# One double-width GpSimd multiply per split unit, in-place even part, bf16 broadcast row

## The chip, the cores and the metric

The kernel runs on one core of a Trainium2 chip. The metric is the device time of one execution in microseconds (us). The core's engines are TensorE (PE in the profile; PEld is its weight load), VectorE (DVE), ScalarE (ACT), GpSimd (POOL) and SyncE (SP, which issues DMAs here). GpSimd works only between SBUF tiles; matmul results lie in PSUM, which VectorE and ScalarE read.

## The reference, cut to what matters

```python
# x: 8 x 3008 x 256; w_gate, w_val: 256 x 1536; w_out: 1536 x 256; all float32
X = np.fft.fft(x, axis=1)
X = np.fft.fft(X, axis=2)
h = X.real.astype(np.float32).reshape(8 * 3008, 256)
g = h @ w_gate
silu = g * (1.0 / (1.0 + np.exp(-g)))
out = (silu * (h @ w_val)) @ w_out
```

The real part of a 2D Fourier transform of real data has a symmetry: row k and row 3008 - k of a batch are the sum and the difference of an even part and an odd part. The kernel computes the two parts once and forms both rows ("plus" and "minus") from them.

## The kernel before, in words

The transform along the sequence is done with matmuls against cosine and sine tables. Its input is first folded to a quarter of its length on GpSimd (`fold_steps`, lines 153 to 172), and the transform's results are put by VectorE (line 580, `put`) into bf16 tiles `Pt` (even part) and `Qt` (odd part). The transform along the 256 columns is multiplied into the weights beforehand (`Wp`, `Wq`, `Wm`).

The columns (sequence positions of all batches) are cut into 24 tiles `t`, of 480, 512 and at the end 320 columns; the hidden width 1536 is cut into 12 slices `f` of 128. A unit is a pair (t, f). All units run in order, and the order on every engine is the order in which the program is written (`manual_schedule`). A turn of the main loop writes `part_a` of a unit, four matmuls of the output stage, `part_b` of the unit before, four more of the output stage, and then what is due there of the folds on GpSimd and of the transforms (`whole_part`).

There are two kinds of unit. In a plain unit, TensorE builds gate `g` and value `v` of the plus rows in PSUM, ScalarE takes the SiLU (line 743), VectorE multiplies (line 744); in `part_b` a further matmul into the same banks turns both into the minus rows, and ScalarE and VectorE repeat the step (lines 761 and 762). In a split unit the value is left as even part `e` and odd part `o`, in two PSUM banks, and VectorE makes both signs from them in three steps: `es` = e plus the broadcast row `bc` times a column of `w0` (line 731), `vp` = es - o/2 (line 733), `vm` = es + o/2, written backwards (line 735). The multiply of SiLU and value is then GpSimd's: the plus rows in `part_a` (line 736), the minus rows in `part_b` (line 758), each behind ScalarE's SiLU of that sign (lines 728 and 757). `bc` is row d=0 of `Qt` spread over all partitions by a matmul, once for each tile (lines 855 to 859).

Tiles 3 to 22 have split units: f = 0, 2, 3, 5, 7, 9 in tiles 3 to 20, and f = 0, 1, 2, 4, 5, 7, 8, 10, 11 in tiles 21 and 22. That makes 126.

The products go to the bf16 tiles `hp` (plus) and `hm` (minus). The output stage (`OWork`, line 676) of a tile starts when its last unit is done and is spread over the next tile's units, eight matmuls to a unit: first the blocks of plus rows, each over f = 0 to 11, then those of minus rows. ScalarE copies the result to `ev`, SyncE writes it out.

PSUM has three banks for `g` (`psG`), three for `v`, `e` and `o` (`psV`), and two for the output stage (`psO`). A bank is free for the next matmul when its last reader is done: for `e` that is line 731, for `o` line 735. In SBUF, the pools `sgv` (SiLU) and `vv` (`vp` and `vm`) have four single buffers each, and `es` two.

Of the kernel before, what the change touches and what calls it, by code (L numbers as in the profile page):

```python
# [12 lines left out]
F32 = mybir.dt.float32  # L13
I32 = mybir.dt.int32
BF16 = mybir.dt.bfloat16
AF = mybir.ActivationFunctionType
Alu = mybir.AluOpType
# [14 lines left out]
def kernel(  # L32
# [8 lines left out]
    nc = tc.nc  # L41
    B, M, D = x.shape
    Dff = moe_w_gate.shape[1]
    P = 128
# [4 lines left out]
    nF = Dff // P  # L49
    T = 512  # L50
# [16 lines left out]
    def width(t):  # L67
        return wide[t]
# [17 lines left out]
    Wo = const.tile([P, nF, D], BF16, name="Wo")  # L86
# [3 lines left out]
    w0 = const.tile([P, nF], F32, name="w0")  # L90
# [169 lines left out]
    for i in range(6):  # L260
        ps = psO.tile([P, T], F32, name="o")
# [252 lines left out]
    def pq_tiles(t):  # L514
        if t not in ptile:
            w = width(t) + B if t == nT - 1 else T
            ptile[t] = (pqp if t < nT - 1 else const).tile([P, w], BF16, name="Pt")
            qtile[t] = (pqp if t < nT - 1 else const).tile([P, w], BF16, name="Qt")
        return ptile[t], qtile[t]
# [94 lines left out]

    hp = ctx.enter_context(tc.tile_pool(name="ht", bufs=2))
    sgp = ctx.enter_context(tc.tile_pool(name="sg", bufs=3))
    sgv = ctx.enter_context(tc.tile_pool(name="sgv", bufs=4))
    esp = ctx.enter_context(tc.tile_pool(name="es", bufs=2))
    bcp = ctx.enter_context(tc.tile_pool(name="bc", bufs=2))
    vvp = ctx.enter_context(tc.tile_pool(name="vv", bufs=4))  # L620
    evp = ctx.enter_context(tc.tile_pool(name="evO", bufs=4))

    def row_pieces(c0, n, minus):


        res = []
        c = c0
        while c < c0 + n:
            if c >= NC:
                res.append((c - c0, c0 + n - c, (c - NC) * M, M))  # L630
                break
            b, r = divmod(c, H)
            for lo, hi, k0 in ((0, GH, 4), (GH, G, H), (G, G + GH, 2), (G + GH, 2 * G, H + 2),
                               (2 * G, 3 * G, 1), (3 * G, 4 * G, H + 1)):
                if lo <= r < hi:
                    break
            e = min(c0 + n, b * H + hi)
            k = k0 + 4 * (r - lo)
            if minus:
                res.append((c0 + n - e, e - c, b * M + M - k - 4 * (e - c - 1), 4))  # L640
            else:
                res.append((c - c0, e - c, b * M + k, 4))
            c = e
        return res

    def rows(r0, n, step):
        return out[r0:r0 + step * (n - 1) + 1:step, :]

    class OWork:
# [21 lines left out]
        def run(self, k):  # L671
            for st, pair, j, minus, c, n, f, hts, t in self.steps[:k]:
                if "ps" not in st:
                    st["ps"] = psO.tile([P, 2, D], F32, name="o")
                ps = st["ps"]
                nc.tensor.matmul(ps[:n, j, :], hts[minus][:, f, c:c + n], Wo[:, f, :],  # L676
                                 start=(f == 0), stop=(f == nF - 1))
                if j == len(pair) - 1 and f == nF - 1:
                    ev = evp.tile([P, 2, D], F32, name="ev")
                    np_ = max(q[2] for q in pair)  # L680
                    if all(q[2] == P for q in pair):
                        nc.scalar.copy(ev[:, 0:len(pair), :], ps[:, 0:len(pair), :])  # L682
                    else:
                        for jj, q in enumerate(pair):
                            nc.scalar.copy(ev[:q[2], jj, :], ps[:q[2], jj, :])
                    for jj, (mi, cc, nn) in enumerate(pair):
                        for p0, cnt, r0, step in row_pieces(t0[t] + (width(t) - cc - nn if mi else cc), nn, mi):
                            nc.sync.dma_start(out=rows(r0, cnt, step),
                                              in_=ev[p0:p0 + cnt, jj, :])
            self.steps = self.steps[k:]  # L690

    units = [(t, f) for t in range(nT) for f in range(nF)]
    hts = {}
    state = {}
# [6 lines left out]
    bc = {}  # L701
# [5 lines left out]
    def part_a(u):  # L707
        t, f = u
        w = width(t) + (B if t == nT - 1 else 0)
        fs = slice(f * P, (f + 1) * P)  # L710
        if f == 0:
            hts[t] = (hp.tile([P, nF, T + B], BF16, name="hp"), hp.tile([P, nF, T], BF16, name="hm"))
        Pt, Qt = pq_tiles(t)

        def mm(ps, Wt, gv, src, start, stop):
            nc.tensor.matmul(ps[:, :w], Wt[:, gv, fs], src[:, :w], start=start, stop=stop,  # L716
                             skip_group_check=True)

        g = psG.tile([P, T], F32, name="g")
        mm(g, Wp, 0, Pt, True, False)  # L720
        mm(g, Wq, 0, Qt, False, True)
        if split(u):
            e = psV.tile([P, T], F32, name="v")
            mm(e, Wp, 1, Pt, True, True)
            o = psV.tile([P, T], F32, name="v")
            mm(o, Wm, 1, Qt, True, True)
            sg = sgv.tile([P, T], F32, name="sgv")
            nc.scalar.activation(sg[:, :w], g[:, :w], AF.Silu)  # L728
            stt = nc.vector.scalar_tensor_tensor
            es = esp.tile([P, T], F32, name="es")  # L730
            stt(es[:, :w], bc[t][:, :w], w0[:, f:f + 1], e[:, :w], op0=Alu.mult, op1=Alu.add)  # L731
            vp = vvp.tile([P, T], F32, name="vv")
            stt(vp[:, :w], o[:, :w], -0.5, es[:, :w], op0=Alu.mult, op1=Alu.add)  # L733
            vm = vvp.tile([P, T], F32, name="vv")
            stt(vm[:, w - 1::-1], o[:, :w], 0.5, es[:, :w], op0=Alu.mult, op1=Alu.add)  # L735
            nc.gpsimd.tensor_tensor(hts[t][0][:, f, :w], sg[:, :w], vp[:, :w], op=Alu.mult)  # L736
            state[u] = (g, vm)
            return
        v = psV.tile([P, T], F32, name="v")
        mm(v, Wp, 1, Pt, True, False)  # L740
        mm(v, Wq, 1, Qt, False, True)
        sg = sgp.tile([P, T], F32, name="sg")
        nc.scalar.activation(sg[:, :w], g[:, :w], AF.Silu)  # L743
        nc.vector.tensor_tensor(hts[t][0][:, f, :w], sg[:, :w], v[:, :w], op=Alu.mult)  # L744
        state[u] = (g, v)

    def part_b(u):
        t, f = u
        w = width(t)
        Pt, Qt = pq_tiles(t)  # L750
        g, v = state.pop(u)
        for gv, ps in ((0, g), (1, v))[:1 if split(u) else 2]:
            nc.tensor.matmul(ps[:, :w], Wm[:, gv, f * P:(f + 1) * P], Qt[:, :w], start=False, stop=True,  # L753
                             skip_group_check=True)
        if split(u):
            sg = sgv.tile([P, T], F32, name="sgv")
            nc.scalar.activation(sg[:, w - 1::-1], g[:, :w], AF.Silu)  # L757
            nc.gpsimd.tensor_tensor(hts[t][1][:, f, :w], sg[:, :w], v[:, :w], op=Alu.mult)  # L758
            return
        sg = sgp.tile([P, T], F32, name="sg")  # L760
        nc.scalar.activation(sg[:, :w], g[:, :w], AF.Silu)  # L761
        nc.vector.tensor_tensor(hts[t][1][:, f, w - 1::-1], sg[:, :w], v[:, :w], op=Alu.mult)  # L762


    slot = {(b, part): max(first_tile[(b, part)] - 1, 0) * nF + 4 for b, part in jobs}
# [10 lines left out]
    for b in range(2, B, 2):  # L776
        u = slot[(b, 0)] - 1
# [41 lines left out]
    for jb in jobs[1:]:  # L819
        u = slot[jb]  # L820
# [30 lines left out]
    for i, u in enumerate(units):  # L851
        t, f = u
        if f == 0 and split((t, SPLIT[0])):
            ps = psG.tile([P, T], F32, name="g")
            w = width(t)
            nc.tensor.matmul(ps[:, :w], sel, pq_tiles(t)[1][:, :w], start=True, stop=True)  # L856
            bc.pop(t - 2, None)
            bc[t] = bcp.tile([P, T], F32, name="bc")
            nc.scalar.copy(bc[t][:, :w], ps[:, :w])
        for fn in before.pop(i, ()):  # L860
            fn()
        if i == 10:
            loads[0:0] = ((("A", 1), fn) for fn in load_a(1, nc.sync))
        run_loads(3)
        part_a(u)
        if owork:
            owork.run(4)
        if prev is not None:
            part_b(prev)
            if prev[1] == nF - 1:  # L870
                owork = OWork(prev[0], hts[prev[0]])
                owork.run(4)
        if owork and not (prev is not None and prev[1] == nF - 1):
            owork.run(4)
        for what, j in fold_at.get(i, ()):
            fold_step(what, j, i)
        for what in act_at.pop(i, ()):
            load_next(what)
        if i in job_at:
            whole_part(*job_at[i])  # L880
        prev = u
# [35 lines left out]
```

## Time and profile before

| what | value |
|---|---|
| time, median of 3 runs | 688.46 us (687.03, 688.46, 688.67) |
| span of the profiled execution | 685.5 us |
| PE busy | 672.8 us, 98% of the span |
| POOL busy | 579.1 us, 84% |
| DVE busy | 514.6 us, 75% |
| ACT busy | 432.9 us, 63% |
| DMA | 52.55 MB, 77 GB/s on average |

The span runs from the first to the last instruction of one profiled execution. The profiled execution's own time is not listed apart from the three runs; their median lies 3.0 us above the span. A row of the timeline gives the start in us, the duration in us, the engine, the line of the kernel, the operation, output<-input with shapes, and how many equal instructions in a row; in brackets, how long the engine had stood idle before it and what released it. A row of the groups gives the number of instructions, their busy time in us and the mean of one in ns, then the idle time before them. In the rows of the stages stand the stretch, its length, and the busy time of PE, PEld, DVE, ACT and POOL with the number of instructions, the granted clock, the DMA share and GB/s.

### The profile page before, as it was taken

What the parts mean: (1) busy time and instruction counts of PE and PEld (TensorE: products, weight loads), DVE (VectorE), ACT (ScalarE), POOL (GpSimd) and SP (SyncE); (2) the same over time, 40 slices, a digit from 0 to 9 for tenths busy, and PEclk for the clock granted to TensorE, in tenths of its full rate; (3) what the DMA queues carried; (4) which work ended last, traced back from release to release, by engine and by line L of the source; (5) the groups of instructions that cost most, each with busy time, mean ns of one, the idle gap of its engine ahead of it and who ended that gap; (6) DMA issues with size and microseconds to landing.
All of it is one profiled execution on the core that took longest, in us unless ns stands there. A gap on an engine that the chain in (4) does not pass through costs nothing.

```text
span 685.5 us, 13259 instructions
## 1 busy us (share of the span) xinstructions
PE 672.8 (98%) x4374; PEld 414.2 (60%) x4374; DVE 514.6 (75%) x919; ACT 432.9 (63%) x764; POOL 579.1 (84%) x565
## 2 busy tenths in 40 slices
PE   8999999999999999999999999999999999999997
PEld 5446655666656566565665566655665656656676
DVE  8896667777777777777777777777786777788862
ACT  7676655666656666565666666655665656656663
POOL 8897987899998999999998989997999555658920
PEclk9999999999999999999999999999999999999999
DMA  9657353324315213335134111125111111101112
GB/s 220 115 77 133 102 138 113 96 76 101 99 32 134 67 51 105 86 71 131 41 76 116 48 32 47 47 58 128 46 48 32 38 40 33 47 31 47 47 48 70
DMA packets 45567, 52.55 MB, mean 77 GB/s; under 512 B 6290, under 2 KB 33466, under 8 KB 45498
## 3 DMA queue, kind: packets, MB, share of 16 engines
q1 hardware_dynamic: 42314, 49.35, 27.4%
q0 software_dynamic: 3184, 2.36, 2.7%
q8 instruction: 34, 0.56, 0.4%
q14 instruction: 35, 0.29, 0.2%
HBM read 29.39 MB, written 24.65 MB: 79 GB/s over the span
## 4 chain that ended last, share of the span: by engine, by line
PE 89%; DVE 5%; issue 2%; POOL 2%; ACT 0%; DVEq 0%; ACTq 0%; POOLq 0%
PE o L676 34%; PE v L716 17%; PE g L716 16%; PE g L753 9%; PE v L753 4%; PE g L567 3%; PE v L567 3%; DVE vv L735 3%; DVE vv L733 1%; PE v L543 1%; PE g L543 1%; PE g L856 1%; PE g L421 1%; PE v L421 1%; PE o L430 0%
## 5 line engine op out<-in xcount | busy, mean ns | idle before, releaser
L736 POOL TENSOR_TENSOR hp<-sgv,vv 128x512 bf16<-128x512 f32 (+1 forms) x126 | 160.1, 1272 | 54.3 <-DVE vv L733 42.4
L676 PE MATMUL o<-Wo,hp 128*128 128x256 bf16 (+2 forms) x1140 | 169.7, 273 | 0.0
L676 PE MATMUL o<-Wo,hm 128*128 128x256 bf16 (+2 forms) x1140 | 169.7, 273 | 0.0
L758 POOL TENSOR_TENSOR hm<-sgv,vv 128x512 bf16<-128x512 f32 (+1 forms) x126 | 159.6, 1272 | 8.5 <-ACT sgv L757 8.1
L676 PEld LDWEIGHTS <-hp 128*128 128x128 bf16 (+2 forms) x1140 | 111.9, 98 | 68.3 <-issue 7.8
L676 PEld LDWEIGHTS <-hm 128*128 128x128 bf16 (+2 forms) x1140 | 111.8, 98 | 64.8 <-issue 4.9
L744 DVE TENSOR_TENSOR hp<-sg,v 128x512 bf16<-128x512 f32 (+2 forms) x162 | 107.9, 666 | 33.2 <-ACT sg L743 32.4
L731 DVE SCALAR_TENSOR_TENSOR es<-bc,w,v 128x512 f32<-128x512 f32 (+1 forms) x126 | 93.7, 744 | 50.5 <-PE v L716 50.3
L762 DVE TENSOR_TENSOR hm<-sg,v 128x512 bf16<-128x512 f32 (+2 forms) x162 | 107.4, 663 | 24.1 <-ACT sg L761 14.4
L761 ACT ACTIVATE sg<-g 128x512 f32<-128x512 f32 (+2 forms) x162 | 94.7, 585 | 45.6 <-PE g L753 45.4
L743 ACT ACTIVATE sg<-g 128x512 f32<-128x512 f32 (+2 forms) x162 | 94.4, 583 | 45.0 <-PE g L716 43.5
L716 PE MATMUL g<-Qt,Wq 128*128 128x512 bf16 (+2 forms) x288 | 108.0, 375 | 0.5 <-DVE Qt L580 0.5
L716 PE MATMUL g<-Pt,Wp 128*128 128x512 bf16 (+2 forms) x288 | 108.1, 376 | 0.1
L716 PE MATMUL v<-Pt,Wp 128*128 128x512 bf16 (+2 forms) x288 | 108.0, 375 | 0.0
L753 PE MATMUL g<-Qt,Wm 128*128 128x512 bf16 (+2 forms) x288 | 108.0, 375 | 0.0
L757 ACT ACTIVATE sgv<-g 128x512 f32<-128x512 f32 (+1 forms) x126 | 75.3, 598 | 47.4 <-PE g L753 41.1
L728 ACT ACTIVATE sgv<-g 128x512 f32<-128x512 f32 (+1 forms) x126 | 75.1, 596 | 40.3 <-PE g L716 35.5
L733 DVE SCALAR_TENSOR_TENSOR vv<-v,es 128x512 f32<-128x512 f32 (+1 forms) x126 | 87.0, 690 | 17.6 <-PE v L753 1.0
L735 DVE SCALAR_TENSOR_TENSOR vv<-v,es 128x512 f32<-128x512 f32 (+1 forms) x126 | 85.7, 680 | 2.7 <-POOL hm L758 2.7
L716 PEld LDWEIGHTS <-Wp 128*128 128x128 bf16 x576 | 56.2, 98 | 41.0 <-issue 4.2
L682 ACT COPY ev<-o 128x512 f32<-128x512 f32 x90 | 52.7, 586 | 30.8 <-PE o L676 28.2
L153 POOL TENSOR_TENSOR SDf<-XA 128x1024 f32<-128x1024 f32 x28 | 66.0, 2364 | 5.2 <-DMA XC<-in_x_dram 3.3
(165 smaller groups left out, 738.0 us busy)
## 6 DMA issues: line engine op xcount, KB each, us to landing
out_dram<-ev SPq DMA_DIRECT2D x96, 128.0 KB
XA<-in_x_dram SPq DMA_DIRECT2D x32, 256.0 KB
XA<-in_x_dram SPq DMA_DIRECT2D x112, 64.0 KB
XC<-in_x_dram SPq DMA_DIRECT2D x32, 120.0 KB
XC<-in_x_dram SPq DMA_DIRECT2D x105, 32.0 KB
out_dram<-ev SPq DMA_DIRECT2D x12, 120.0 KB
out_dram<-ev SPq DMA_DIRECT2D x10, 112.0 KB
XA<-in_x_dram SPq DMA_DIRECT2D x1, 1024.0 KB
```

The lines of the kernel that those rows point to most:

```text
L676: nc.tensor.matmul(ps[:n, j, :], hts[minus][:, f, c:c + n], Wo[:, f, :], start=(f == 0), stop=(f == nF - 1))
L716: nc.tensor.matmul(ps[:, :w], Wt[:, gv, fs], src[:, :w], start=start, stop=stop, skip_group_check=True)
L731: stt(es[:, :w], bc[t][:, :w], w0[:, f:f + 1], e[:, :w], op0=Alu.mult, op1=Alu.add)
L733: stt(vp[:, :w], o[:, :w], -0.5, es[:, :w], op0=Alu.mult, op1=Alu.add)
L735: stt(vm[:, w - 1::-1], o[:, :w], 0.5, es[:, :w], op0=Alu.mult, op1=Alu.add)
L736: nc.gpsimd.tensor_tensor(hts[t][0][:, f, :w], sg[:, :w], vp[:, :w], op=Alu.mult)
L743: nc.scalar.activation(sg[:, :w], g[:, :w], AF.Silu)
L744: nc.vector.tensor_tensor(hts[t][0][:, f, :w], sg[:, :w], v[:, :w], op=Alu.mult)
L753: nc.tensor.matmul(ps[:, :w], Wm[:, gv, f * P:(f + 1) * P], Qt[:, :w], start=False, stop=True, skip_group_check=True)
L758: nc.gpsimd.tensor_tensor(hts[t][1][:, f, :w], sg[:, :w], v[:, :w], op=Alu.mult)
L761: nc.scalar.activation(sg[:, :w], g[:, :w], AF.Silu)
L762: nc.vector.tensor_tensor(hts[t][1][:, f, w - 1::-1], sg[:, :w], v[:, :w], op=Alu.mult)
```

## The change

- `hp` and `hm` become one tile `hpm` with an axis for the sign.
- `sg` and `vv` of a split unit hold both signs in one tile, with three such buffers each (before: four single ones).
- GpSimd multiplies both signs in one instruction of 2 x 512 columns, in `part_b`. Only for f = 10 and 11 (split in tiles 21 and 22 alone) the plus rows keep an instruction of their own in `part_a`.
- The pool `es` is gone: the even part is written to the plus half of `vv`; then the minus half is made from it, and then the plus half in place. The minus step thus comes second and the plus step third.
- `bc` is bf16 instead of float32.
- Output buffers `ev`: three instead of four.

Line numbers behind the edits fall by one or two: 731 becomes 730, 733 and 735 become 732 and 731 (plus and minus change places), 758 becomes 757, 676 becomes 675.

```diff
-    sgv = ctx.enter_context(tc.tile_pool(name="sgv", bufs=4))
-    esp = ctx.enter_context(tc.tile_pool(name="es", bufs=2))
+    sgv = ctx.enter_context(tc.tile_pool(name="sgv", bufs=3))
...
-    vvp = ctx.enter_context(tc.tile_pool(name="vv", bufs=4))
-    evp = ctx.enter_context(tc.tile_pool(name="evO", bufs=4))
+    vvp = ctx.enter_context(tc.tile_pool(name="vv", bufs=3))
+    evp = ctx.enter_context(tc.tile_pool(name="evO", bufs=3))
...
-                nc.tensor.matmul(ps[:n, j, :], hts[minus][:, f, c:c + n], Wo[:, f, :],
+                nc.tensor.matmul(ps[:n, j, :], hts[:, minus, f, c:c + n], Wo[:, f, :],
...
-            hts[t] = (hp.tile([P, nF, T + B], BF16, name="hp"), hp.tile([P, nF, T], BF16, name="hm"))
+            hts[t] = hp.tile([P, 2, nF, T], BF16, name="hpm")
...
-            sg = sgv.tile([P, T], F32, name="sgv")
-            nc.scalar.activation(sg[:, :w], g[:, :w], AF.Silu)
+            sg = sgv.tile([P, 2, T], F32, name="sgv")
+            nc.scalar.activation(sg[:, 0, :w], g[:, :w], AF.Silu)
             stt = nc.vector.scalar_tensor_tensor
-            es = esp.tile([P, T], F32, name="es")
-            stt(es[:, :w], bc[t][:, :w], w0[:, f:f + 1], e[:, :w], op0=Alu.mult, op1=Alu.add)
-            vp = vvp.tile([P, T], F32, name="vv")
-            stt(vp[:, :w], o[:, :w], -0.5, es[:, :w], op0=Alu.mult, op1=Alu.add)
-            vm = vvp.tile([P, T], F32, name="vv")
-            stt(vm[:, w - 1::-1], o[:, :w], 0.5, es[:, :w], op0=Alu.mult, op1=Alu.add)
-            nc.gpsimd.tensor_tensor(hts[t][0][:, f, :w], sg[:, :w], vp[:, :w], op=Alu.mult)
-            state[u] = (g, vm)
+            vv = vvp.tile([P, 2, T], F32, name="vv")
+            stt(vv[:, 0, :w], bc[t][:, :w], w0[:, f:f + 1], e[:, :w], op0=Alu.mult, op1=Alu.add)
+            stt(vv[:, 1, w - 1::-1], o[:, :w], 0.5, vv[:, 0, :w], op0=Alu.mult, op1=Alu.add)
+            stt(vv[:, 0, :w], o[:, :w], -0.5, vv[:, 0, :w], op0=Alu.mult, op1=Alu.add)
+            if f >= nF - 2:
+                nc.gpsimd.tensor_tensor(hts[t][:, 0, f, :w], sg[:, 0, :w], vv[:, 0, :w], op=Alu.mult)
+            state[u] = (g, (sg, vv))
             return
...
-            sg = sgv.tile([P, T], F32, name="sgv")
-            nc.scalar.activation(sg[:, w - 1::-1], g[:, :w], AF.Silu)
-            nc.gpsimd.tensor_tensor(hts[t][1][:, f, :w], sg[:, :w], v[:, :w], op=Alu.mult)
+            sg, vv = v
+            nc.scalar.activation(sg[:, 1, w - 1::-1], g[:, :w], AF.Silu)
+            m = slice(1 if f >= nF - 2 else 0, 2)
+            nc.gpsimd.tensor_tensor(hts[t][:, m, f, :w], sg[:, m, :w], vv[:, m, :w], op=Alu.mult)
             return
...
-            bc[t] = bcp.tile([P, T], F32, name="bc")
+            bc[t] = bcp.tile([P, T], BF16, name="bc")
```

More of the change, by code (lines that the diff above doesn't have):

```diff
@@ L743, in part_a @@
         nc.scalar.activation(sg[:, :w], g[:, :w], AF.Silu)
-        nc.vector.tensor_tensor(hts[t][0][:, f, :w], sg[:, :w], v[:, :w], op=Alu.mult)
+        nc.vector.tensor_tensor(hts[t][:, 0, f, :w], sg[:, :w], v[:, :w], op=Alu.mult)
         state[u] = (g, v)
@@ L761, in part_b @@
         nc.scalar.activation(sg[:, :w], g[:, :w], AF.Silu)
-        nc.vector.tensor_tensor(hts[t][1][:, f, w - 1::-1], sg[:, :w], v[:, :w], op=Alu.mult)
+        nc.vector.tensor_tensor(hts[t][:, 1, f, w - 1::-1], sg[:, :w], v[:, :w], op=Alu.mult)
     slot = {(b, part): max(first_tile[(b, part)] - 1, 0) * nF + 4 for b, part in jobs}
```

## The prediction

> **What bounds the kernel now.** I read the page first: busy shares, granted clock, the chain that ended last.
>
> ```profile
> span 685.5 us, 13259 instructions
> PE 672.8 (98%) x4374; PEld 414.2 (60%) x4374; DVE 514.6 (75%) x919; ACT 432.9 (63%) x764; POOL 579.1 (84%) x565
> PEclk9999999999999999999999999999999999999999
> PE 89%; DVE 5%; issue 2%; POOL 2%; ACT 0%; DVEq 0%; ACTq 0%; POOLq 0%
> PE o L676 34%; PE v L716 17%; PE g L716 16%; PE g L753 9%; PE v L753 4%; PE g L567 3%; PE v L567 3%; DVE vv L735 3%; DVE vv L733 1%; PE v L543 1%; PE g L543 1%; PE g L856 1%; PE g L421 1%; PE v L421 1%; PE o L430 0%
> ```
>
> TensorE at full clock sets the time. The change leaves every matmul and its order alone, so it can only move the moments at which TensorE waits. One other line stands out in the chain: `vv L735`, the third VectorE step of a split unit. I then asked the stages, since the change is on GpSimd.
>
> ```profile
> 120.00:420.00 300.00, 298.62 (x1937) 182.87 (x1935) 230.43 (x403) 190.33 (x335) 288.84 (x266) 1.00 0.30 79
> 540.00:600.00 60.00, 59.81 (x393) 37.03 (x391) 45.92 (x82) 38.98 (x68) 33.21 (x27) 1.00 0.14 41
> ```
>
> The last busy column before the clock is POOL: 96% while folds run (tiles 3 to 13), 55% behind them. POOL is close to the bound in the middle, and PE (the first column) is as full there as later. Last I looked in the timelines for the place where L735 meets TensorE, in tile 9, units f=2 and f=3.
>
> ```profile
> 274.02 0.38 PE L716 MATMUL v<-Pt,Wp 128*128 128x512 bf16 x1
> 274.24 0.38 PE L716 MATMUL v<-Qt,Wm 128*128 128x512 bf16 x1
> ...
> 276.19 0.38 PE L716 MATMUL v<-Pt,Wp 128*128 128x512 bf16 x1
> 276.67 0.38 PE L716 MATMUL v<-Qt,Wm 128*128 128x512 bf16 x1
> ```
>
> ```profile
> 274.44 0.75 DVE L731 SCALAR_TENSOR_TENSOR es<-bc,w,v 128x512 f32<-128x512 f32 x1 [0.73 <-PE v L716]
> 275.32 0.69 DVE L733 SCALAR_TENSOR_TENSOR vv<-v,es 128x512 f32<-128x512 f32 x1
> 275.93 0.68 DVE L735 SCALAR_TENSOR_TENSOR vv<-v,es 128x512 f32<-128x512 f32 x1
> 276.53 0.68 DVE L762 TENSOR_TENSOR hm<-sg,v 128x512 bf16<-128x512 f32 x1
> 277.12 0.74 DVE L731 SCALAR_TENSOR_TENSOR es<-bc,w,v 128x512 f32<-128x512 f32 x1
> ```
>
> Two split units stand side by side. Matmuls start 0.22 us apart (274.02, 274.24), but f=3's odd matmul comes 0.48 behind its even one: it needs the bank of f=2's odd part, free when L735 ends (275.93 + 0.68 = 276.61). So 0.26 us is lost, and the chain behind it starts with the even matmul at 274.02 and runs through all three VectorE steps without slack. The same gap is in each of tiles 3 to 20 once (f=2, 3) and six times in tiles 21 and 22: 24 in all, of which these are the first and the last.
>
> ```profile
> 111.98 0.36 PE L716 MATMUL v<-Pt,Wp 128*128 128x480 bf16 x1
> 112.39 0.36 PE L716 MATMUL v<-Qt,Wm 128*128 128x480 bf16 x1
> ...
> 650.77 0.38 PE L716 MATMUL v<-Pt,Wp 128*128 128x512 bf16 x1
> 651.25 0.38 PE L716 MATMUL v<-Qt,Wm 128*128 128x512 bf16 x1
> ```
>
> These 24 stalls, about 6 us, are nearly all that TensorE loses behind the start, and most that any change here could win.
>
> **The change, part by part.** First VectorE. The three steps stay three and the odd bank is still freed by the third; but that step now writes the even row in place, after the second has read it. In the built program it waits for the second's semaphore, where before both only read `es`. I need the price of such a wait.
>
> ```profile
> 5.90 1.37 DVE L306 SCALAR_TENSOR_TENSOR rr<-kf,mM,t 128x377 f32<-128x377 f32 x2
> 7.31 0.82 DVE L310 TENSOR_SCALAR ra<-rr 128x754 int32<-128x754 int32 x1
> ```
>
> L310 waits directly for the L306 in front of it and starts 0.04 us after its end (5.90 + 1.37 = 7.27). L735, with no such wait, starts 0.08 before the end of L733 (275.32 + 0.69 = 276.01, against 275.93). So the wait costs 0.12 us. The upper bound is the existing es-to-vv step, 275.32 against 274.44 + 0.75 = 275.19: 0.13 behind the end, so 0.21. I take 0.12, since L310's is the same single wait; es-to-vv waits for several things.
>
> On this, the Trainium skill's page "VectorE: DVE Perf Modes", section "The DRAIN you can't avoid", says that a semaphore between VectorE instructions costs nothing extra, as the pipeline drains anyway. The rows above disagree; by it this term would be nothing.
>
> Second, the first step. It writes `vv` directly, so it waits for GpSimd (the product three split units back) as well as for the matmul: a separate wait instruction comes in front. A VectorE step with such a pair, L580, against PE:
>
> ```profile
> 282.87 0.49 PE L567 MATMUL g<-Tab,BBc 64*128 64x376 bf16 x2
> ...
> 283.47 0.61 DVE L580 TENSOR_TENSOR Qt<-g,od 128x304 bf16<-128x304 f32 x2 [0.62 <-PE g L567]
> ```
>
> It starts 0.11 us after the matmuls' end; the es row above started 0.04 after its own (274.02 + 0.38 = 274.40). So I take 0.06 more, bounds 0 and 0.09 (the 0.13 of es-to-vv, less 0.04). Behind the waiting step stand the rest of VectorE's queue and, through the banks, TensorE; with three double buffers the product it needs is three split units old, so GpSimd itself rarely holds it.
>
> Both lie on the chain of the 24 pairs: 24 x (0.12 + 0.06) = 4.3 us, bounds 24 x 0.12 = 2.9 and 24 x (0.21 + 0.09) = 7.2. In the other 102 split units the 0.18 is hidden: VectorE idles before a later step (0.73 us in the 274.44 row). Were that cover gone they would cost as much each, 18 us.
>
> Third, the bf16 row.
>
> ```profile
> L744 DVE TENSOR_TENSOR hp<-sg,v 128x512 bf16<-128x512 f32 (+2 forms) x162 | 107.9, 666 | 33.2 <-ACT sg L743 32.4
> L731 DVE SCALAR_TENSOR_TENSOR es<-bc,w,v 128x512 f32<-128x512 f32 (+1 forms) x126 | 93.7, 744 | 50.5 <-PE v L716 50.3
> L733 DVE SCALAR_TENSOR_TENSOR vv<-v,es 128x512 f32<-128x512 f32 (+1 forms) x126 | 87.0, 690 | 17.6 <-PE v L753 1.0 <-POOL hp L736 0.3
> L735 DVE SCALAR_TENSOR_TENSOR vv<-v,es 128x512 f32<-128x512 f32 (+1 forms) x126 | 85.7, 680 | 2.7 <-POOL hm L758 2.7
> ```
>
> One bf16 side beside f32 ones brings nothing (L744, 666 ns, against 680 and 690): 0 for L731, and 0 for the copy that writes `bc`.
>
> Fourth, GpSimd: 126 + 126 products become 122 double ones and four pairs.
>
> ```profile
> L736 POOL TENSOR_TENSOR hp<-sgv,vv 128x512 bf16<-128x512 f32 (+1 forms) x126 | 160.1, 1272 | 54.3 <-DVE vv L733 42.4
> L758 POOL TENSOR_TENSOR hm<-sgv,vv 128x512 bf16<-128x512 f32 (+1 forms) x126 | 159.6, 1272 | 8.5 <-ACT sgv L757 8.1
> L153 POOL TENSOR_TENSOR SDf<-XA 128x1024 f32<-128x1024 f32 x28 | 66.0, 2364 | 5.2 <-DMA XC<-in_x_dram 3.3
> L163 POOL TENSOR_TENSOR Af<-EOf 128x516 f32<-128x516 f32 (+1 forms) x22 | 24.2, 1102 | 0.5
> ```
>
> One of 1024 columns lies between 2 x 1102 = 2.2 and 2 x 1272 = 2.54 us; L153 has that size at 2.36, but f32 out. I take 2.5, twice the product with its own types: GpSimd's work stays as it is. The saved instruction is small, and even 0.3 x 122 = 37 us saved there would not shorten TensorE's work.
>
> The Trainium skill's "GPSIMD Engine Reference", section "Performance versus the Vector engine", has 4497 ns for 2048 f32 columns; an estimate from it is 2.25 us, and by it GpSimd would gain some 30 us and the next term would go, leaving about 692.4 in all.
>
> What does move is the plus product. It was queued ahead of its unit's minus one; now both come at the minus one's place. TensorE's output stage reads plus rows first, and f=9 in the third group of four, one unit after the tile ends. When did the minus products of f=9 end, against that?
>
> ```profile
> 162.36 1.29 POOL L758 TENSOR_TENSOR hm<-sgv,vv 128x512 bf16<-128x512 f32 x1
> ...
> 302.13 1.28 POOL L758 TENSOR_TENSOR hm<-sgv,vv 128x512 bf16<-128x512 f32 x1
> ```
>
> ```profile
> 162.43 0.60 PE L676 MATMUL o<-Wo,hp 128*128 128x256 bf16 x4
> ...
> 301.79 0.60 PE L676 MATMUL o<-Wo,hp 128*128 128x256 bf16 x4
> ```
>
> For tiles 4 and 9 the minus product ends at 163.65 and 303.41, about 1.2 and 1.6 us after TensorE starts the group that now needs it. Up to that instruction GpSimd's queue holds the same work in both kernels, and it runs without a gap there, so it cannot finish earlier. That is 2.8 us, less some 0.7 as TensorE's slower pairs let GpSimd catch up, plus some 0.4 as GpSimd can no longer start on plus products early: 2.5 us, bounds 0 (if the double is shorter) and 5 (another 1.3 us product in each of the two). In the other tiles the product of f=9 ends before its group starts.
>
> Last, one gain.
>
> ```profile
> 139.87 0.38 PE L716 MATMUL v<-Pt,Wp 128*128 128x512 bf16 x1
> 140.69 0.38 PE L716 MATMUL v<-Qt,Wm 128*128 128x512 bf16 x1 [0.44 <-DVE vv L735]
> ```
>
> This pair of tile 4 waits 0.82, not 0.48: L733 was held for a `vv` buffer. Three double buffers hold one unit more than four singles, so 0.35 is won. The output's `ev` has three buffers instead of four, so a copy waits for an earlier write.
>
> ```profile
> 676.44 0.58 ACT L682 COPY ev<-o 128x512 f32<-128x512 f32 x1 [1.97 <-PE o L676]
> ...
> 681.85 0.36 ACT L685 COPY ev<-o 64x256 f32<-64x256 f32 x1 [0.89 <-PE o L676]
> ```
>
> Copies are closest at the end: there the last now needs the write of the third before it, begun at 677.02, 4.8 us earlier. The last write of all, begun at 682.2, has landed when the span ends at 685.5, so one takes at most 3.3: 0, at worst 1 us. ScalarE, SyncE and the DMAs keep their order: 0. The start (tiles 0 to 2) has no split unit: 0.
>
> **Sum.** 4.3 + 2.5 - 0.35 = 6.45 us on the span, 685.5 to 692. The median of the runs is 688.46, 3.0 above the span; with the same 3.0 the forecast is 694.9 us.
>
> **Rivals.** *The wait is free.* VectorE may empty its pipeline between any two instructions, so that a wait for the one in front adds nothing. For it: L735 has never been seen with such a wait. Against: the L310 and es-to-vv rows. It leaves 24 x 0.06 = 1.4, less 0.35, and, with the double at its lower bound, no late product: 688.46 + 1.05 = 689.5, no change to speak of. Chance 0.12. The Trainium skill's "VectorE: DVE Perf Modes", in the section named above, states this case.
>
> *The first step gets shorter with its bf16 row.* Then the chain of the pairs shrinks: it decides when L731 falls below 0.744 - 0.18 = 0.56 us. At half, 0.37, each stall shrinks by 0.19, 24 x 0.19 = 4.6, and the late products give back 2.5: 688.46 - 4.6 + 2.5 - 0.35 = 686.0, faster. Against: L744. Chance 0.09.
>
> *GpSimd becomes the bound.* If the double takes over 2.7 us instead of 2.5, the 11 folded tiles with 6 each add 0.2 x 66 = 13 us against 300 - 288.84 = 11 of idle there; at 2.9 they add 26, so TensorE is 15 late, with the other waits inside that: 688.46 + 15 = 703.5. Against: L153 at 2.36. Chance 0.10.
>
> The forecast has the remaining 0.69.
>
> **Numbers.** About 0.3%, 2 us, is what a measurement can tell here. Faster: the second rival and little else, 0.09. Same (686.4 to 690.5): the first, and a forecast with all terms at their lower ends, 0.13. Slower 0.78. The range: 689.5 (all waits at their least, no late product) to 700.3 (688.46 + 7.2 + 5 - 0.35).
>
> **What would show it.** Right: in the 24 pairs the odd matmul starts 0.6 to 0.7 us behind the even one instead of 0.48; the second-to-third VectorE start goes from 0.61 to 0.73; the double product is 2.5 us; weight loads of `hpm` wait for POOL in tiles 4 and 9. Wrong: 0.61 unchanged, L730 well under 0.74, or PE waiting for POOL in most tiles.

## The result and the profile after

| kernel | median of the runs | span of the profiled execution |
|---|---|---|
| before | 687.96 us (687.03 to 688.67, 4 runs) | 685.5 us |
| after | 694.10 us (693.41 to 695.12, 4 runs) | 692.3 us |

The changed kernel is slower: ratio 1.0088, 95% interval 1.0076 to 1.0100, that is 6.1 us. The forecast was 694.9 us and a span of 692.0.

First the page of the changed kernel: busy shares, clock and the chain that ended last.

```profile
span 692.3 us, 13022 instructions
PE 674.3 (97%) x4374; PEld 415.2 (60%) x4374; DVE 526.0 (76%) x919; ACT 433.4 (63%) x764; POOL 562.6 (81%) x443
PE 80%; DVE 9%; POOL 4%; DMA 4%; issue 2%; SPq 1%; ACT 0%; DVEq 0%; POOLq 0%; ACTq 0%
```

TensorE does the same 4374 matmuls. GpSimd has 122 instructions fewer and 16.5 us less to do (562.6 against 579.1), and none of it reaches the end. In the chain VectorE's share went from 5 to 9% and GpSimd's from 2 to 4%. What TensorE waits for (engine, line, what it waited for; then us in total, times, longest) names both:

```profile
PE v L715 <- DVE vv L732: 6.7, 24, 0.6
PE o L675 <- POOL hpm L757: 1.4, 1, 1.4
```

The first row is new as a group: before, there was one such wait of 0.4 us, in tile 4; at the other pairs TensorE stood idle for about 0.10 us (0.48 less the 0.38 of a matmul), which is too short for this list. It is the 24 pairs of split units side by side. Here is the pair of tile 9 again, TensorE's matmuls and VectorE's steps from the timeline:

```profile
280.06 0.38 PE L715 MATMUL v<-Pt,Wp 128*128 128x512 bf16 x1
280.71 0.38 PE L715 MATMUL v<-Qt,Wm 128*128 128x512 bf16 x1 [0.27 <-DVE vv L732]
```

```profile
277.90 0.38 PE L715 MATMUL v<-Pt,Wp 128*128 128x512 bf16 x1
...
278.39 0.75 DVE L730 SCALAR_TENSOR_TENSOR vv<-bc,w,v 128x512 f32<-128x512 bf16 x1 [0.69 <-PE v L715]
279.25 0.69 DVE L731 SCALAR_TENSOR_TENSOR vv<-v,vv 128x512 f32<-128x512 f32 x1
279.97 0.69 DVE L732 SCALAR_TENSOR_TENSOR vv<-v,vv 128x512 f32<-128x512 f32 x1
```

The odd matmul comes 0.65 us behind the even one (0.48 before). The steps show where from. The third starts 0.72 behind the second, 0.03 after its end at 279.94, instead of 0.61. The first starts 0.11 after the end of its matmul at 278.28, instead of 0.04. The second starts 0.86 behind the first, instead of 0.88. By the median over all split units these are 0.73, 0.12 and 0.85.

The second wait is the plus product of f=9 in tile 4, which now comes in the double instruction (timeline, GpSimd and TensorE):

```profile
162.91 2.37 POOL L757 TENSOR_TENSOR hpm<-sgv,vv 128x1024 bf16<-128x1024 f32 x1
...
163.70 0.27 PE L675 MATMUL o<-Wo,hpm 128*128 128x256 bf16 x1
165.34 0.50 PE L675 MATMUL o<-Wo,hpm 128*128 128x256 bf16 x3 [1.36 <-POOL hpm L757]
```

The double ends at 165.28 and TensorE, which had come to f=9 at about 163.8, starts at 165.34.

**How the 6.1 us add up.** One thing has to be taken out first: in 8 of the 14 profiled executions here, of kernels made from either one, TensorE's clock is cut for a few microseconds at the start, and all that follows is some 1.4 us later. The stages (stretch, its length, busy time of the five engines with the instructions, granted clock, DMA share, GB/s) show it between 13 and 17 us, for the execution before and the one after:

```profile
13.00:17.00 4.00, 3.96 (x18) 2.03 (x18) 2.74 (x6) 3.83 (x8) 3.82 (x8) 1.00 1.37 171
```

```profile
13.00:17.00 4.00, 3.95 (x15) 2.12 (x15) 2.67 (x6) 3.92 (x8) 3.83 (x8) 0.60 1.34 172
```

So from here on the stretch from the first matmul of tile 0 to the first of tile 23 is compared, which leaves that start out ("the body"). Its ends before and after:

```profile
25.19 0.36 PE L716 MATMUL g<-Pt,Wp 128*128 128x480 bf16 x1
652.55 0.30 PE L716 MATMUL g<-Pt,Wp 128*128 128x328 bf16 x1
```

```profile
26.49 0.36 PE L715 MATMUL g<-Pt,Wp 128*128 128x480 bf16 x1
659.40 0.30 PE L715 MATMUL g<-Pt,Wp 128*128 128x328 bf16 x1
```

The body takes 632.92 us instead of 627.36, 5.55 more. The 6.1 us between the medians are more than that because the two sets of runs hold the two starts in different numbers, by their times two of four before and three of four after the slower one. Like with like, the kernel before has a median of 688.6 us over the runs with a mean granted clock of 0.996 or 0.997 in all sessions; three of the four runs after have 0.997 and a median of 694.1, which is 5.5 more. The time that the odd matmuls of the 24 pairs start later than 0.217 us behind their even ones adds up to 10.61 us instead of 6.47: 4.1 of the 5.55. Tile 4's late product is 1.5: tile 5, from its first matmul to the next tile's, takes 30.14 us instead of 28.43, of which 0.18 are its pair. No other tile moved by more than 0.1 us beyond its pairs.

### The profile page after: what moved, and what is told of

Read it like the earlier page. It is cut to its first block, busy times and chain, and to the rows that moved or that the text cites. A ratio compares the mean times of both kernels' runs of the same rounds, so it can differ in the third digit from the quotient of the medians.

```text
span 692.3 us, 13022 instructions
## 1 busy us (share of the span) xinstructions
PE 674.3 (97%) x4374; PEld 415.2 (60%) x4374; DVE 526.0 (76%) x919; ACT 433.4 (63%) x764; POOL 562.6 (81%) x443
## 3 DMA queue, kind: packets, MB, share of 16 engines
q1 hardware_dynamic: 42314, 49.35, 26.5%
## 4 chain that ended last, share of the span: by engine, by line
PE 80%; DVE 9%; POOL 4%; DMA 4%; issue 2%; SPq 1%; ACT 0%; DVEq 0%; POOLq 0%; ACTq 0%
PE o L675 31%; PE v L715 15%; PE g L715 15%; PE g L751 7%; PE v L751 4%; PE g L567 3%; DMA XC<-in_x_dram 3%; PE v L567 3%; DVE vv L731 3%; DVE vv L730 3%; DVE vv L732 2%; POOL hpm L757 2%; POOL SDf L153 1%; DMA XA<-in_x_dram 1%; DVE hpm L742 1%
## 5 line engine op out<-in xcount | busy, mean ns | idle before, releaser
L757 POOL TENSOR_TENSOR hpm<-sgv,vv 128x1024 bf16<-128x1024 f32 (+2 forms) x126 | 291.8, 2321 | 78.1 <-ACT sgv L755 70.4
L675 PE MATMUL o<-Wo,hpm 128*128 128x256 bf16 (+3 forms) x2280 | 339.3, 273 | 1.4 <-POOL hpm L757 1.4
L675 PEld LDWEIGHTS <-hpm 128*128 128x128 bf16 (+3 forms) x2280 | 223.7, 98 | 138.6 <-issue 16.8
L742 DVE TENSOR_TENSOR hpm<-sg,v 128x512 bf16<-128x512 f32 (+2 forms) x162 | 107.6, 664 | 30.8 <-ACT sg L741 29.1
L730 DVE SCALAR_TENSOR_TENSOR vv<-bc,w,v 128x512 f32<-128x512 bf16 (+1 forms) x126 | 93.7, 743 | 48.9 <-PE v L715 43.7
L761 DVE TENSOR_TENSOR hpm<-sg,v 128x512 bf16<-128x512 f32 (+2 forms) x162 | 107.3, 662 | 23.7 <-ACT sg L760 14.1
L731 DVE SCALAR_TENSOR_TENSOR vv<-v,vv 128x512 f32<-128x512 f32 (+1 forms) x126 | 87.0, 690 | 13.5 <-DVE vv L730 0.5
L732 DVE SCALAR_TENSOR_TENSOR vv<-v,vv 128x512 f32<-128x512 f32 (+1 forms) x126 | 86.9, 690 | 4.3
L153 POOL TENSOR_TENSOR SDf<-XA 128x1024 f32<-128x1024 f32 x28 | 66.0, 2363 | 8.2 <-DMA XC<-in_x_dram 2.9
L751 PE MATMUL v<-Qt,Wm 128*128 128x512 bf16 (+2 forms) x162 | 60.2, 372 | 2.0 <-DVE hpm L742 2.0
L715 PE MATMUL v<-Qt,Wq 128*128 128x512 bf16 (+2 forms) x162 | 60.2, 372 | 0.0
L715 PEld LDWEIGHTS <-Wq 128*128 128x128 bf16 x450 | 44.0, 98 | 24.6 <-issue 0.6
```

Of the source, the lines that this page charges most:

```text
L675: nc.tensor.matmul(ps[:n, j, :], hts[:, minus, f, c:c + n], Wo[:, f, :], start=(f == 0), stop=(f == nF - 1))
L730: stt(vv[:, 0, :w], bc[t][:, :w], w0[:, f:f + 1], e[:, :w], op0=Alu.mult, op1=Alu.add)
L731: stt(vv[:, 1, w - 1::-1], o[:, :w], 0.5, vv[:, 0, :w], op0=Alu.mult, op1=Alu.add)
L732: stt(vv[:, 0, :w], o[:, :w], -0.5, vv[:, 0, :w], op0=Alu.mult, op1=Alu.add)
L742: nc.vector.tensor_tensor(hts[t][:, 0, f, :w], sg[:, :w], v[:, :w], op=Alu.mult)
L757: nc.gpsimd.tensor_tensor(hts[t][:, m, f, :w], sg[:, m, :w], vv[:, m, :w], op=Alu.mult)
```

## The experiments

Twelve kernels, each against the kernel before in the same session. Bodies are worked out as above; they are of one profiled execution each and free of the start, so where a median and a body differ, the argument goes by the body.

| kernel | median us (range, runs) | ratio to before, 95% interval | body us | against before |
|---|---|---|---|---|
| after | 694.10 (693.41 to 695.12, 4) | 1.0088, 1.0076 to 1.0100 | 632.92 | +5.55 |
| even part apart | 689.64 (688.70 to 690.44, 8) | 1.0027, 1.0017 to 1.0037 | 629.15 | +1.79 |
| plus from minus | 692.89 (692.61 to 694.08, 4) | 1.0078, 1.0065 to 1.0092 | 632.74 | +5.38 |
| in place alone | 695.47 (693.78 to 695.48, 4) | 1.0104, 1.0088 to 1.0121 | 634.20 | +6.84 |
| f=9 single | 692.64 (691.05 to 692.67, 5) | 1.0067, 1.0054 to 1.0079 | 631.39 | +4.03 |
| bc float32 | 693.61 (692.88 to 694.18, 4) | 1.0079, 1.0065 to 1.0093 | 632.90 | +5.54 |
| apart, f=9 single | 688.48 (686.78 to 688.51, 12) | 1.0000, 0.9991 to 1.0009 | 627.23 | -0.13 |
| alternate, before | 688.91 (687.31 to 689.09, 11) | 1.0008, 1.0000 to 1.0017 | 627.78 | +0.42 |
| alternate, after | 687.88 (687.41 to 689.11, 12) | 0.9999, 0.9991 to 1.0008 | 627.83 | +0.47 |
| odd, before | 689.48 (687.81 to 691.13, 12) | 1.0024, 1.0013 to 1.0034 | 628.21 | +0.85 |
| odd, after | 692.52 (691.50 to 696.62, 6) | 1.0076, 1.0054 to 1.0097 | 634.88 | +7.52 |
| odd, apart | 691.40 (689.27 to 691.92, 6) | 1.0046, 1.0032 to 1.0059 | 629.39 | +2.03 |
| odd from tile 10 | 686.61 (685.23 to 688.48, 12) | 0.9981, 0.9972 to 0.9991 | 626.13 | -1.23 |

**The even part apart.**

```diff
+    esp = ctx.enter_context(tc.tile_pool(name="es", bufs=2))
...
-            stt(vv[:, 0, :w], bc[t][:, :w], w0[:, f:f + 1], e[:, :w], op0=Alu.mult, op1=Alu.add)
-            stt(vv[:, 1, w - 1::-1], o[:, :w], 0.5, vv[:, 0, :w], op0=Alu.mult, op1=Alu.add)
-            stt(vv[:, 0, :w], o[:, :w], -0.5, vv[:, 0, :w], op0=Alu.mult, op1=Alu.add)
+            es = esp.tile([P, T], F32, name="es")
+            stt(es[:, :w], bc[t][:, :w], w0[:, f:f + 1], e[:, :w], op0=Alu.mult, op1=Alu.add)
+            stt(vv[:, 1, w - 1::-1], o[:, :w], 0.5, es[:, :w], op0=Alu.mult, op1=Alu.add)
+            stt(vv[:, 0, :w], o[:, :w], -0.5, es[:, :w], op0=Alu.mult, op1=Alu.add)
```

> The changed kernel with the even part in a tile of its own again (two es buffers), so that no VectorE step reads what the one in front wrote except through es, and the first step no longer waits for GpSimd; the double product stays. Theory (two waits on the chain of the 24 side-by-side split pairs): VectorE's second-to-third start goes from 0.73 back to 0.61, the odd matmul from 0.65 behind the even one to 0.48, 24 x 0.175 = 4.2 us off, to about 689.9. Rival (the waits are free, the loss is GpSimd's later products): the pairs and VectorE's steps may move, but the time stays at 694.1.

The pair of tile 9, from the timeline:

```profile
279.00 0.38 PE L716 MATMUL v<-Pt,Wp 128*128 128x512 bf16 x1
279.47 0.38 PE L716 MATMUL v<-Qt,Wm 128*128 128x512 bf16 x1
```

Back to 0.47 and 689.64, as expected: without the two waits the pairs cost what they did before. The minus step is still the second here, so the new order of the steps is not what costs the time. The body is 3.77 shorter than that of the changed kernel and 1.79 above that of before, and TensorE's waits for GpSimd say why it is not level with before. They are now two, and tile 9's is new:

```profile
165.34 0.50 PE L676 MATMUL o<-Wo,hpm 128*128 128x256 bf16 x3 [1.16 <-POOL hpm L759]
...
305.28 0.50 PE L676 MATMUL o<-Wo,hpm 128*128 128x256 bf16 x3 [0.42 <-POOL hpm L759]
```

In the changed kernel TensorE's slower pairs hid this one: there the double of tile 9 ended at 305.75 and the matmuls began at 305.84.

**Plus rows made from the minus rows.** As the kernel in front, with one line changed, so that the third step alone waits for the second and the first has no wait for GpSimd:

```diff
-            stt(vv[:, 0, :w], o[:, :w], -0.5, es[:, :w], op0=Alu.mult, op1=Alu.add)
+            stt(vv[:, 0, :w], o[:, :w], -1.0, vv[:, 1, w - 1::-1], op0=Alu.mult, op1=Alu.add)
```

> As the kernel with the even part apart, but the third step makes the plus rows from the minus rows of the second (vm - o), so that it alone waits for the step in front, and the first step has no wait for GpSimd. Theory (0.12 us for the wait between the steps, 0.06 for the pair of waits of the first): second-to-third start 0.73, pairs 0.60, 24 x 0.12 = 2.9 us slower than with the even part apart, about 692.8. Rival (the pair of waits of the first step costs it all): pairs 0.48, 689.9. Rival (the wait between the steps costs it all): pairs 0.65, 694.1.

```profile
280.02 0.38 PE L716 MATMUL v<-Pt,Wp 128*128 128x512 bf16 x1
280.62 0.38 PE L716 MATMUL v<-Qt,Wm 128*128 128x512 bf16 x1 [0.22 <-DVE vv L734]
```

0.60 in the pairs, second-to-third start 0.73, median 692.89: neither 0.47 nor 0.65. The wait for the instruction in front is worth 0.12 us, the rest of the 0.17 belongs to the first step. The body is 3.6 us longer than with the even part apart: 3.1 in the pairs, the rest in later products of f=9.

**In place alone.** The kernel before, with the order and the in-place write of the changed one, four single `vv` buffers and single products:

```diff
-            es = esp.tile([P, T], F32, name="es")
-            stt(es[:, :w], bc[t][:, :w], w0[:, f:f + 1], e[:, :w], op0=Alu.mult, op1=Alu.add)
             vp = vvp.tile([P, T], F32, name="vv")
-            stt(vp[:, :w], o[:, :w], -0.5, es[:, :w], op0=Alu.mult, op1=Alu.add)
+            stt(vp[:, :w], bc[t][:, :w], w0[:, f:f + 1], e[:, :w], op0=Alu.mult, op1=Alu.add)
             vm = vvp.tile([P, T], F32, name="vv")
-            stt(vm[:, w - 1::-1], o[:, :w], 0.5, es[:, :w], op0=Alu.mult, op1=Alu.add)
+            stt(vm[:, w - 1::-1], o[:, :w], 0.5, vp[:, :w], op0=Alu.mult, op1=Alu.add)
+            stt(vp[:, :w], o[:, :w], -0.5, vp[:, :w], op0=Alu.mult, op1=Alu.add)
```

> The kernel before with the in-place even part alone: first step writes the plus tile, minus step second, plus step third in place; GpSimd's products stay single, bc stays float32. Theory: pairs 0.65 as in the changed kernel, 24 x 0.175 = 4.2 us slower than before, about 692.2; no weight load of a product waits for POOL in tile 4. Rival (the loss needs GpSimd's double product): no change, 688.0.

```profile
278.74 0.38 PE L716 MATMUL v<-Pt,Wp 128*128 128x512 bf16 x1
279.42 0.38 PE L716 MATMUL v<-Qt,Wm 128*128 128x512 bf16 x1 [0.30 <-DVE vv L734]
...
645.51 0.38 PE L716 MATMUL v<-Pt,Wp 128*128 128x512 bf16 x1
646.43 0.38 PE L716 MATMUL v<-Qt,Wm 128*128 128x512 bf16 x1 [0.54 <-DVE vv L734]
```

The loss needs no double product, so that rival falls, but the size was missed: 695.47 against 692.2. The pairs are 0.68, as the second step still takes a buffer of its own here and starts 0.88 behind the first (0.85 after). And in tile 22 the odd matmuls of f=4 and f=5 come 0.92 behind (the second is shown): the interval from tile 22 to 23 is 26.87 us against 25.37 after and 24.84 before. In tile 9 a matmul of the transform waits another 0.65 us for the third step. Four single buffers hold two units, three double ones three, which fits a first step that waits for GpSimd; by itself it was not tried. So the double `vv` buffers, which were counted with 0.35 us in tile 4, probably spared the changed kernel this too.

**f=9's plus product on its own.** `nF - 2` becomes `nF - 3` in `part_a` and `part_b`.

> The changed kernel with the plus product of f = 9 also as an instruction of its own in part_a, as those of f = 10 and 11. Theory: the wait of the output stage in tile 5 for the product of f = 9 (1.4 and 1.7 us by the waits) goes, 1.5 us off, about 692.6; pairs stay at 0.65. Rival (the late product is hidden by what is late next): 694.1. If two singles of f = 9 cost GpSimd more than the double (2 x 1.27 against 2.32, 20 times 0.2 us), tiles 4 to 9 keep waiting for it elsewhere.

692.64. TensorE's waits have no row with a product of GpSimd any more, and the body is 1.53 shorter than that of the changed kernel. The late product was worth what the trace showed.

**Both undone, the double product kept for all f below 9.**

> The changed kernel with the even part apart and the f = 9 plus product on its own: both terms of the prediction undone, the double product kept for the other f. Theory: 694.1 - 4.2 - 1.5 = 688.4, no more than 0.5 us from the kernel before. Rival (something else in the change costs time too, such as the three output buffers or the slower start of the profiled execution): clearly above 688.4.

688.48, ratio 1.0000 (0.9991 to 1.0009), body 0.13 below that of before. The two terms are the whole loss. What is left of the change (doubles, bf16 row, fewer output buffers) neither costs nor gains anything that these runs can tell (0.1%).

**The broadcast row in float32 again.** `bc` is declared `F32` in the changed kernel.

> The changed kernel with the broadcast row in float32 again. Theory: the bf16 row neither costs nor gains; the first step stays at 743 ns, the time at 694.1 (0 +- 0.5 us). Rival (the bf16 row is read faster or slower): the first step moves from 743 ns, and 24 pairs with it, 24 x the difference.

The groups of the first step (count, busy us, mean ns), in the changed kernel and in this one:

```profile
L730 DVE SCALAR_TENSOR_TENSOR vv<-bc,w,v 128x512 f32<-128x512 bf16 (+1 forms) x126 | 93.7, 743 | 48.9 <-PE v L715 43.7 <-POOL hpm L757 4.9 <-ACT bc L858 0.2
```

```profile
L730 DVE SCALAR_TENSOR_TENSOR vv<-bc,w,v 128x512 f32<-128x512 f32 (+1 forms) x126 | 93.7, 744 | 48.8 <-PE v L715 44.0 <-POOL hpm L757 4.2 <-POOL EOf L157 0.3
```

743 against 744 ns, and the same body to 0.02 us.

**No pairs: alternate units.** `SPLIT = (0, 2, 4, 6, 8, 10)` in both kernels.

> The kernel before with the split units of tiles 3 to 20 at f = 0, 2, 4, 6, 8, 10 instead of 0, 2, 3, 5, 7, 9, so that no two stand side by side there; the same number of products. Theory (the stall belongs to the side-by-side pair): 18 of the 24 pairs go, 18 x 0.26 = 4.7 us off, about 683.3. Rival (the stall moves to the plain unit behind, or GpSimd's products of f = 10 are late for the output stage): 688 or more.

> The changed kernel with the split units of tiles 3 to 20 at f = 0, 2, 4, 6, 8, 10. The waits of 0.12 and 0.06 us stay on VectorE in all 126 units, but 18 of the 24 pairs are gone. Theory (the waits cost time in the pairs alone): 18 x 0.43 = 7.8 us off, about 686.3, and 684.8 if the late product of f = 9 goes too (f = 10 keeps an instruction of its own in part_a). Rival (each wait costs its 0.18 us in all units, or GpSimd's double of f = 8 and the product of f = 10 are late): above 690.

The first was missed: 688.91, not 683.3. The 18 pairs did go: over all split units, the odd matmuls come 1.5 us late in sum instead of 7.3 (1.6 instead of 6.5 in the pairs, the rest at f=0). But the time came back at the seam, where one tile ends and the next begins. Around the end of tile 15, TensorE and ScalarE of the kernel with alternate units:

```profile
463.74 0.38 PE L753 MATMUL g<-Qt,Wm 128*128 128x512 bf16 x1
...
464.39 0.38 PE L856 MATMUL g<-Qt,sel 128*128 128x512 bf16 x1
464.87 0.38 PE L716 MATMUL g<-Pt,Wp 128*128 128x512 bf16 x1
...
464.22 0.60 ACT L757 ACTIVATE sgv<-g 128x512 f32<-128x512 f32 x1 [0.55 <-PE g L753]
```

and of the kernel before:

```profile
461.86 0.38 PE L753 MATMUL v<-Qt,Wm 128*128 128x512 bf16 x1
...
462.51 0.38 PE L856 MATMUL g<-Qt,sel 128*128 128x512 bf16 x1
462.73 0.38 PE L716 MATMUL g<-Pt,Wp 128*128 128x512 bf16 x1
```

The broadcast (`sel`) takes one of the three gate banks. The next tile's first gate matmul then needs the bank of f=10, which ScalarE reads until 464.82, and starts 0.48 behind the broadcast instead of 0.22. Before, f=10 was a plain unit, whose further matmul (461.86) covered that time. That is 18 x 0.26 = 4.7 of the 5.8 won, and some 1.5 go to the products of f=10, late in tiles 4 and 9.

In the changed kernel alternate units give 687.88, level with before, and a body 5.1 us shorter than that of the changed kernel. That is short of the 684.8 to 686.3 expected, for the same reason, but it decides the question it was for: the waits stand in all 126 split units, and where no two of them are side by side no cost shows. Of the two kernels with alternate units the changed one loses 1.0 us more in the six pairs left, and wins 1.0 at the 18 seams: there ScalarE's minus SiLU of f=10 starts 0.04 us behind its matmul instead of 0.10, since it writes a buffer that the unit already holds and no longer waits for GpSimd.

**Odd units.** `SPLIT = (1, 3, 5, 7, 9, 11)`, which leaves plain units on both sides of the seam; on the kernel before, on the changed kernel with f=9 single, and on that with the even part apart.

> The kernel before with the split units of tiles 3 to 20 at f = 1, 3, 5, 7, 9, 11: none side by side, and plain ones at f = 10 and f = 0, around the broadcast's matmul at the seam of two tiles. In the kernel with split units at 0, 2, ... 10 the 0.26 us won at each pair came back there: the first matmul of the next tile waits for the gate bank of f = 10, and the seam's turn takes 2.43 instead of 2.38 with one matmul less. Theory (that is all of it): 18 x 0.26 = 4.7 us off and nothing comes back in tiles 11 to 20; in tiles 4 to 9 the products of f = 9 and 11 may be late for the output stage by up to 3 us: 683 to 686. Rival (the stall moves once more, to the turn behind f = 11): 687 or more.

> The changed kernel with the split units of tiles 3 to 20 at f = 1, 3, 5, 7, 9, 11 and single products for f = 9, 10, 11. Theory: as with the kernel before, since the waits of 0.12 and 0.09 us cost nothing where no pair stands side by side: 683 to 686 and 1.0 us (6 pairs of tiles 21 and 22 at 0.18) more. Rival (the double products are late once more): 688 or more.

> As the one in front, with the even part in a tile of its own. Theory: the 6 pairs of tiles 21 and 22 lose 0.48 instead of 0.65, 1.0 us less; the rest equal. Rival (the in-place wait costs in every split unit): 120 x 0.18 = 21 us less, or a part of it.

All three missed. Behind the folds it works: tiles 17 to 19 take 24.94, 28.32 and 28.12 us, 0.31 less each than before. But the plus product of f=11 comes one unit too late for the output stage where GpSimd is full. TensorE's waits for it, of the kernel before with odd units:

```profile
PE o L676 <- POOL hp L736: 5.5, 5, 2.4
```

On the changed kernel, and on that with the even part apart, where f=9 and 11 have two single products each, the row reads:

```profile
PE o L675 <- POOL hpm L734: 9.1, 6, 2.5
```

```profile
PE o L676 <- POOL hpm L736: 6.6, 5, 1.9
```

For the last rival: odd units with and without the in-place write differ by 5.5 us in the body, of which 1.1 are in the pairs of tiles 21 and 22 and 2.5 in these waits for GpSimd. Nearly all the rest, 1.7, lies in tile 5. Both kernels wait 1.9 us there for the product of f=11, but in the execution with the in-place write TensorE's granted clock then falls, and in the other it doesn't. The stage behind that wait, with the in-place write:

```profile
167.00:171.00 4.00, 4.00 (x17) 2.07 (x15) 0.69 (x1) 1.19 (x2) 3.90 (x5) 0.57 0.45 125
```

and with the even part apart:

```profile
167.00:171.00 4.00, 4.00 (x28) 2.63 (x27) 1.95 (x3) 2.54 (x5) 3.92 (x5) 1.00 0.50 124
```

So of the 5.5 us some 0.2 are left for a cost in every split unit, against the 21 of the rival.

**Odd units from tile 10 on, kernel before.**

```diff
+    SPLIT_ODD = (1, 3, 5, 7, 9, 11)
...
-        return 3 <= u[0] < nT - 1 and u[1] in (SPLIT if u[0] < t_end else SPLIT_END)
+        return 3 <= u[0] < nT - 1 and u[1] in (SPLIT if u[0] < 10 else SPLIT_ODD if u[0] < t_end else SPLIT_END)
...
-        if f == 0 and split((t, SPLIT[0])):
+        if f == 0 and 3 <= t < nT - 1:
```

The last of these lines keeps the broadcast row for tiles whose f=0 is not split.

> The kernel before with the split units at f = 1, 3, 5, 7, 9, 11 in tiles 10 to 20 only; tiles 3 to 9 keep 0, 2, 3, 5, 7, 9. With the odd places in all tiles, the tiles behind the folds took 24.94, 28.33 and 28.12 us instead of 25.25, 28.63 and 28.43, and what was lost lay in tiles 3 to 5, 9 and 10, where the plus product of f = 11 came late. Theory: 11 x 0.31 = 3.4 us off, less 0.5 for late products that were seen in tiles 13 and 15: 685 (684.5 to 686), faster than both kernels. Rival (GpSimd falls behind in tiles 10 to 15 here too): 687 or more.

```profile
PE o L676 <- POOL hp L737: 1.5, 2, 1.3
```

686.61, ratio 0.9981 (0.9972 to 0.9991): faster than both kernels by a little, above the 684.5 to 686 expected. Tile 10 is still among the folds, and its product of f=11 held TensorE for 1.3 us.

## Why the prediction was right, point by point

- **Which work the change touches.** Right: TensorE does the same, and what was taken from GpSimd did not shorten the end. GpSimd's share of work in the folded stretch fell, and PE's with it, since the pairs take longer and one product comes late:

```profile
120.00:420.00 300.00, 295.57 (x1915) 180.81 (x1915) 232.90 (x399) 188.16 (x331) 277.28 (x198) 1.00 0.29 79
```

- **The third step's wait, 0.12.** Right: second-to-third start 0.61 to 0.73 after, and in the kernel that has this wait alone. The Trainium skill's "VectorE: DVE Perf Modes", section "The DRAIN you can't avoid", holds that such a semaphore costs nothing extra; these runs do not agree, 0.12 us each. The rival built on it (689.5) is out.
- **The first step's pair of waits, 0.06.** Measured 0.12 instead of 0.04 behind the matmul, so 0.08; but the second step, which no longer takes a buffer, starts 0.03 earlier. Together 0.17 to 0.18 per pair, as predicted. The two small errors cancelled, as the in-place kernel with single buffers (0.68) shows.
- **24 pairs and no other place.** Right: 4.1 us including tile 4's gain of 0.35, predicted 4.3 - 0.35 = 3.95. That they agree so closely is partly luck, since tile 8 adds 0.35 that wasn't foreseen. There the first step of f=2 starts 0.47 us behind its matmul instead of 0.11, and the pair takes 1.00:

```profile
254.29 0.38 PE L715 MATMUL v<-Pt,Wp 128*128 128x512 bf16 x1
255.29 0.38 PE L715 MATMUL v<-Qt,Wm 128*128 128x512 bf16 x1 [0.62 <-DVE vv L732]
```

  It is there in the kernels whose first step waits for GpSimd with double buffers (1.00 to 1.02) and gone with the even part apart (0.47). But the product three split units back had ended 8 us earlier, so what held this one step stays open.
- **The bf16 row, 0.** Right: 743 against 744 ns. The rival of the shorter first step (686.0) is out.
- **The double product, 2.5 us.** Too high. The groups by shape:

```profile
L757 POOL TENSOR_TENSOR hpm<-sgv,vv 128x1024 bf16<-128x1024 f32 x116 | 273.4, 2362 | 69.5 <-ACT sgv L755 61.7 <-DVE vv L731 7.7
L734 POOL TENSOR_TENSOR hpm<-sgv,vv 128x512 bf16<-128x512 f32 x4 | 5.1, 1272 | 3.3 <-DVE vv L732 3.3
```

  2362 ns, the same as the fold's L153 with float32 out; the row with the same size was the better guide than twice the row with the same types. One double is 2 x 1272 - 2362 = 182 ns shorter than two singles, and GpSimd's busy time fell by 16.5 us, where the forecast had none. "GpSimd becomes the bound" (703.5) thereby fell away.
- **The late product of f=9, 2.5 us.** This is the term that was mis-sized: 1.5 us, in tile 4 alone. Tile 9's double ended just in time, because it is shorter and the pairs had put TensorE back. The estimate by the Trainium skill's "GPSIMD Engine Reference", section "Performance versus the Vector engine" (2.25 us, and no late product), was nearer to 2362 ns than the forecast's 2.5, but its end did not follow: the product is late because it is moved, not because it is slow.
- **Output buffers and the rest, 0.** Right, by the kernel with both terms undone.

Of 6.45 us predicted for the span, 5.55 are found in the body; that the spans still agree (692.0 and 692.3) owes 1.3 us to the slower start of that one execution, which is luck. The 3.0 us that the forecast put between span and median hold such a start too: in every run that lists both, the time lies 1.7 to 1.9 us above the span. The 694.9 thus stood for a run with the slower start, as three of the four after it were. The low end of the range, 689.5, is the first rival's time and not the sum of the lower bounds, which is 688.46 + 2.9 - 0.35 = 691.0; the measured time lies above both.

## What to carry to other kernels

Before fusing instructions on an engine that is nearly full but not the bound, look at what the fusion moves: the product that comes later, the wait that a shared or in-place buffer adds, and the chain on which these stand. Here a saved buffer that made an engine wait for its own last result delayed the step by 0.12 us at each place, and that mattered only where the next unit needed the bank at once. And a stall that is taken from one place has to be looked for at the next tight one: the gate banks at the seam took back most of what the pairs had given.

## What the runs showed of the hardware

- A VectorE step that waits for the one in front of it started 0.12 us later than one that doesn't (0.73 against 0.61, medians over 126). A wait for a second engine at a step that waits for TensorE anyway took 0.08 us (0.12 against 0.04 behind the matmul's end). On ScalarE the minus SiLU of a split unit started 0.10 us behind its matmul with such a second wait, before, and 0.04 without it, after (medians over 126).
- A GpSimd multiply of 1024 columns takes 2362 ns with bf16 out, two of 512 take 2544 ns.
- The start of TensorE differs between executions. With a granted clock of 0.57 to 0.60 between 13 and 17 us, tile 0 begins at 26.5 to 26.6 us; with 1.00, at 24.9 to 25.3. Of the 14 profiled executions here 8 were of the first kind, among them kernels made from either one; and the runs of the kernel before fall apart alike, with a median of 688.6 us at a mean clock of 0.996 or 0.997 and 687.3 at 0.999 or 1.0. The Trainium skill's "TensorE: Matmul & The Clock Gate", Part 1, states that the windows in which the clock gate watches TensorE's activity run free of the kernel's start, so that the slow part varies from run to run; the rows agree as far as they go, since they show the variation and not the windows. It is 1.4 us here, as much as the smaller terms of this case, so terms of that size are better read from the stretch behind the start than from one span.
